# Two sliding-window attention layers and two spatial-shift MLPs on one core: alternating parities over the partitions, one transfer per tile, and most activations turned by a DMA instead of TensorE

## The chip, the cores and the metric

The kernel runs on one core of one Trainium2 chip. The metric is the device time of one execution in microseconds (us); lower is better. Three executions of the kernel before took 1238.16, 1242.08 and 1244.62 us, so its median is 1242.08 us. Everything is read from one profiled execution, whose first instruction starts 1238.3 us before its last one ends.

## The reference, cut to what matters

```python
def A(x):                      # x: [2048, 512]; wqkv [512,1536], wo [512,512]
    q, k, v = split_heads(layernorm(x) @ wqkv)      # 32 heads of 16
    # position s looks at s, s-2, s-4, ..., s-14 (8 of them), masked below 0
    return softmax(q . k[window] / 4) . v[window] @ wo
def B(x):                      # F = 1792
    h = gelu(layernorm(x) @ w1)
    # the four quarters of the features come from positions s-1, s+1, s-2, s+2
    x1 = x + shifted(h) @ w2
    return x1 + gelu(layernorm(x1) @ w3) @ w4
for _ in range(2):
    x = x + A(layernorm(x)) ; x = x + B(layernorm(x))
```

Inputs and outputs are float32. The layer norm stands once in the loop and once more inside A and B; the kernel folds the two into one scale.

## The kernel before, in words

**Work units.** The 2048 positions are cut into 4 blocks of 512 (`NB`), and each block into 4 tiles of 128 positions (`NT`). A unit of the program is a layer and a block, `n` from 0 to 7: 0 to 3 are the blocks of the first pass, 4 to 7 those of the second. A unit goes through five stages:

- `p1_stream(n)` (line 771; the first unit has its own `p1_quarters`, line 727, on plain float32 weights): norm of each tile, the tile turned so that features lie on partitions, then q, k and v by TensorE, evicted to `ev` and written to DRAM (`q_d`, `kv_d`).
- `p2_unit(n, qt)` (line 938): attention for one quarter of the heads: q and k/v are read back from DRAM in a layout in which a partition holds 4 positions of its own and the 7 earlier ones of the window, and VectorE does the products, sums and the softmax. The result `o` is turned into `oT`.
- `p3(n)` (line 1037): `oT` times wo, added to x; norm; the tile turned into `nT`; `nT` times w1, GELU, result `h` with the positions on the free axis, and copies of its edges for the shifts.
- `p4(n)` (line 1153): shifted `h` times w2, added; norm; the tile turned into `x2T` (again a buffer of kind `nT`).
- `p5(n)` (line 1219): 14 chunks of w3, GELU, w4, accumulated in the four `acc` banks of PSUM; the result is added to x and, in the second pass, written out.

**Numbers in two halves.** Except for the first unit, whose weights are used in float32, each float32 operand is held as two float16 numbers, high and low, and every product is three matmuls (`HLS`, line 51: high x high, high x low, low x high). So an activation that has been turned must also be split into a high and a low float16 half.

**Turning a tile.** `turn_pe` (line 644) transposes a 128x512 float32 tile on TensorE, as four 128x128 matmuls with the identity matrix `ident` into one PSUM bank of kind `mm`. `split` (line 667) then has ScalarE copy the bank to float16 (the high half) and VectorE subtract that from the bank (the low half). There are 128 such turns: 4 tiles in each of 8 units at four places, p1, p2 (one for each quarter of the heads), p3 and p4 (7 of them by `turn_f32`, line 656, into plain float32, in the first unit).

**Layout of positions.** In a tile, partitions 0 to 63 hold 64 positions of even parity and 64 to 127 those of odd parity. A transfer between DRAM and such a tile therefore comes as two DMAs of 64 partitions (`dma2`, line 477, `rows`, line 511; the stores of k and v in `p1_stream`, line 798; the output, line 1292). For unit 0, k and v of the first quarter are shifted inside SBUF by small DMAs, and those of the other quarters are copied within SBUF and shifted (lines 952 to 966).

**Order of the work.** Each step is recorded as an operation with its reads, writes and one or more engines that could do it (`op`, line 205). `plan` (line 246) simulates the engines with costs written beside each operation and a list of priorities, `PLACES` (line 57), takes the best operation that is ready, gives buffers from pools (`slots`, line 391), and so fixes the order on every engine; `InOrder` (line 348) keeps the instructions of each engine in that order. All instructions are issued from one helper line, 358, so that the profile tells groups apart by tile names, not by lines. Almost all DMAs are issued by SyncE (SP), in order: a DMA whose buffer is not free yet holds all those behind it.

Of the kernel before, what the change touches and what calls it, by code (L numbers as in the profile page):

```python
# [18 lines left out]
P = 128  # L19
# [11 lines left out]
PAD = W - 1  # L31
NSL = NT + W - 1
# [6 lines left out]

# [4 lines left out]


PLACES = [int(k) for k in """
# [127 lines left out]
""".split()]  # L185


class Buf:

# [11 lines left out]
class Graph:  # L201
# [3 lines left out]
    def __call__(self, key, alts, r=(), w=(), after=(), xfer=0.0):  # L205
# [26 lines left out]
        for p in before:  # L232
            p.succ.append(o)
# [1104 lines left out]
```

## Time and profile before

| what | value |
|---|---|
| times of three executions | 1238.16, 1242.08, 1244.62 us |
| span of the profiled execution | 1238.3 us, 15802 instructions |
| TensorE (PE) busy | 1193.5 us, 5676 matmuls; weight loads 592.2 us beside it |
| VectorE (DVE) busy | 903.5 us |
| ScalarE (ACT) busy | 632.0 us |
| GpSimd (POOL) busy | 372.4 us |
| moved by DMA | 176.71 MB, 143 GB/s over the span |

A group of the profile is read like this: engine, operation, the tile written `<-` the tiles read, shapes, `x`count, then the summed busy time in us and the mean of one in ns, then the idle time of the engine just ahead of them with what ended it. Matmuls overlap in the array, so that their mean duration is longer than the time from one to the next; the price of a matmul in a stream is taken from the starts of neighbours in the timeline. In the chain of waits a piece is a start, a length and what ran or was waited for. The three executions differ by 0.5%.

### The profile page before, as it was taken

The numbers are of one execution on the slowest core, as the hardware profiler recorded it, in microseconds if no ns is written. First come the engines' busy times: TensorE is split into PE (matmuls) and PEld (weight loads), VectorE is DVE, ScalarE is ACT, GpSimd is POOL, SyncE is SP. The second block draws the span as 40 slices with busy tenths as digits, with TensorE's granted clock in tenths as the row PEclk, the third lists the DMA queues.
The fourth block names the chain that finished last, engine by engine and source line by source line (L and its number), as shares of the span: only waits on it lengthen the run. The fifth ranks groups of instructions, "written<-read, shape, count | busy, mean of one in ns | idle before, by whom it ended". The sixth has DMA issues, their size and how long they took to land.

```text
span 1238.3 us, 15802 instructions
## 1 busy us (share of the span) xinstructions
PE 1193.5 (96%) x5676; PEld 592.2 (48%) x5676; DVE 903.5 (73%) x896; ACT 632.0 (51%) x1108; POOL 372.4 (30%) x516
## 2 busy tenths in 40 slices
PE   9977799899999999999999999989999999999998
PEld 7533344455454445444444545444454444444554
DVE  4776998998999989599954998389855888314212
ACT  4645547533774456556543655365543654444431
POOL 6342123402540264147422252051513432121000
PEclk9988899899999999999999999999999999999999
DMA  6565777586666543653348623764157435211322
GB/s 199 160 163 156 220 219 227 161 227 169 195 178 177 132 136 81 151 154 95 109 147 197 162 75 126 202 153 124 60 153 187 124 93 167 68 60 58 88 85 68
DMA packets 129597, 176.71 MB, mean 143 GB/s; under 512 B 11504, under 2 KB 72912, under 8 KB 129520
## 3 DMA queue, kind: packets, MB, share of 16 engines
q1 hardware_dynamic: 127216, 173.78, 50.2%
q10 hardware_dynamic: 2304, 1.95, 0.6%
q8 instruction: 44, 0.72, 0.3%
q14 instruction: 33, 0.27, 0.1%
HBM read 132.64 MB, written 37.87 MB: 138 GB/s over the span
## 4 chain that ended last, share of the span: by engine, by line
PE 76%; DVE 7%; DMA 7%; ACT 3%; POOL 2%; SPq 2%; issue 2%; ACTq 0%; DVEq 0%; POOLq 0%
PE mm L358 54%; PE acc L358 22%; DVE prod L358 3%; SPq L358 2%; DMA kv<-kv_d 2%; DMA kv<-x 1%; DVE L L358 1%; POOL b L358 1%; DMA w<-in_A_x_dram 1%; POOL a L358 1%; DMA h<-in_B_w_dram 1%; ACT junk L358 1%; DMA q<-q_d 1%; ACT ev L358 1%; DMA kv_d<-ev 1%
## 5 line engine op out<-in xcount | busy, mean ns | idle before, releaser
L358 PE MATMUL acc<-w,g 128*128 128x512 f16 (+1 forms) x1260 | 309.0, 394 | 0.0
L358 PE MATMUL mm<-nT,w 128*128 128x512 f16 (+1 forms) x1288 | 305.5, 390 | 1.5 <-ACT nT L358 0.7
L358 PE MATMUL mm<-wq_hl,xt 128*128 128x512 f16 x1008 | 234.8, 389 | 13.3 <-ACT ev L358 11.4
L358 ACT ACTIVATE mm<-mm,s_w 128x512 f32<-128x512 f32 (+1 forms) x144 | 90.6, 629 | 228.8 <-PE mm L358 228.5
L358 PEld LDWEIGHTS <-w 128*128 128x128 f16 x1344 | 124.9, 98 | 137.3 <-issue 1.3
L358 PEld LDWEIGHTS <-g 128*128 128x128 f16 x1176 | 115.1, 98 | 129.9 <-issue 1.1
L358 PEld LDWEIGHTS <-xt 128*128 128x128 f16 x1008 | 100.3, 100 | 133.8 <-issue 23.2
L358 DVE TENSOR_TENSOR prod<-kv,q 128x4096 f32<-128x4096 f32 x29 | 128.6, 4434 | 20.2 <-DMA kv<-kv_d 12.2
L358 DVE TENSOR_TENSOR prod<-kv,L 128x4096 f32<-128x4096 f32 x32 | 141.4, 4418 | 0.6 <-DMA kv<-kv_d 0.3
L358 DVE TENSOR_REDUCE L<-prod 128x256 f32<-128x4096 f32 x32 | 141.2, 4414 | 0.1
L358 DVE TENSOR_TENSOR prod<-prod 128x2048 f32<-128x2048 f32 x64 | 117.5, 1837 | 1.1
L358 POOL TENSOR_TENSOR g<-f,g 128x512 f16<-128x512 f32 x42 | 61.0, 1453 | 189.7 <-ACT g L358 89.4
L358 DVE SCALAR_TENSOR_TENSOR g<-mm,c_g,g 128x512 f16<-128x512 f32 x56 | 41.8, 747 | 75.8 <-ACT g L358 74.1
L358 PE MATMUL mm<-nT,w_hl 128*128 128x512 f16 x384 | 87.8, 379 | 0.0
L358 PE MATMUL mm<-wo_hl,oT 128*128 128x512 f16 x384 | 86.1, 379 | 0.0
L358 PE MATMUL mm<-w_hl,h 128*128 128x512 f16 x384 | 85.0, 379 | 0.0
L358 POOL COPY h<-h 128x126 f16<-128x126 f16 (+3 forms) x56 | 47.4, 869 | 118.1 <-DVE h L358 116.6
L358 PE MATMUL mm<-ident,f 128*128 128x128 f32 x384 | 59.0, 280 | 21.0 <-ACT f L358 16.0
L358 ACT ACTIVATE g<-mm,c_g 128x512 f16<-128x512 f32 x98 | 66.9, 685 | 2.1
L358 PEld LDWEIGHTS mm<-ident,f 128*128 128x128 f32 x384 | 47.2, 143 | 40.2 <-ACT f L358 19.1
L358 ACT ACT_TABLE_LOAD x48 | 61.6, 1283 | 9.0 <-DVE mx L358 5.2
L358 PEld LDWEIGHTS <-oT 128*128 128x128 f16 x426 | 41.7, 98 | 49.4 <-issue 0.6
(159 smaller groups left out, 1365.0 us busy)
## 6 DMA issues: line engine op xcount, KB each, us to landing
w<-w SPq DMA_DIRECT2D x196, 256.0 KB
kv<-kv_d SPq DMA_DIRECT2D x112, 352.0 KB
w<-in_B_w_dram SPq DMA_DIRECT2D x56, 256.0 KB
kv_d<-ev SPq DMA_DIRECT2D x112, 128.0 KB
x<-x SPq DMA_DIRECT2D x32, 256.0 KB
q_d<-ev SPq DMA_DIRECT2D x28, 256.0 KB
w<-g SPq DMA_DIRECT2D x28, 256.0 KB
q<-q_d SPq DMA_DIRECT2D x28, 256.0 KB
```

Of the source, the lines that this page charges most:

```text
L358: i = f(*a, **k).ins
```

## The change

**Parities alternate over partitions.** Partition 2k holds an even and 2k+1 an odd position. A tile of 128 rows is then one access pattern and one DMA, for x, the residual, k and v, and the output:

```diff
-    def rows(ap, b, i, par):
-        r = 512 * b + 2 * i + par
-        v = ap[r:r + 1, 0:D]
-        return bass.AP(tensor=v.tensor, offset=v.offset, ap=[[8 * D, 64], [1, D]])
+    def rows(ap, b, i):
+        v = ap[512 * b + 2 * i:512 * b + 2 * i + 1, 0:D]
+        return at(v, [[8 * D, 64], [D, 2], [1, D]])
```

q, k and v share one DRAM tensor for each pass, `kvq_d`, with 12 planes of 4 + 512 rows of 512 numbers. A k or v tile is read as rows p-4, p-2 and p, so it holds 12 slots of 128 numbers instead of 11, by one DMA instead of two. For unit 0 the quarters 1 to 3 are also written to `kvq_d` and read back; the copies inside SBUF remain for the first quarter alone, three for k and three for v. The edge copies of `h` are strided accordingly.

**Turning by DMA.** A new helper splits first, in SBUF, and turns both halves (128 x 1024 float16, 256 KB) by one transposing DMA from SP's queue:

```diff
+    def turn_dma(key, n, dst, cells, out, rd, scale=None):
+        hl = Buf("g")
...
+        act(key, lambda: A.activation(hv(0), n.t, AF.Copy, scale=sc), rd + k, [(hl, 0), (dst, "new")],
+            also=[(DVE, lambda: V.tensor_scalar(hv(0), n.t, sc, None, ALU.mult), None)])
+        if scale is None:
+            op(key, [(DVE, lambda: V.tensor_sub(hv(1), n.t, hv(0)), None),
+                     (POOL, lambda: G.tensor_sub(hv(1), n.t, hv(0)), None)], [n, (hl, 0)], [(hl, 1)])
+        else:
+            rest(key, lambda: hv(1), lambda: n.t, sc, lambda: hv(0), [n, (hl, 0), scale], [(hl, 1)])
+        op(key, [(SP, lambda: Y.dma_start_transpose(out(), hl.t), None)], [(hl, [0, 1])], hc)
+    MINUS = (1, 2, 3), (0, 1), ()
+    BY_DMA = (4, 5, 6, 7), (2, 3, 4, 5, 6, 7), (1, 2, 3, 4, 5, 6, 7), (2, 3, 4, 5, 6, 7)
```

The four tuples of `BY_DMA` are the units in which p1, p3, p4 and p2 turn by DMA: 16, 24, 29 and 24 turns, 93 of the 128. In `MINUS` stand the units of p1 and p3 (12 and 8 turns) whose turn stays on TensorE with another way to the low half: one more matmul subtracts the high half in the PSUM bank, and ScalarE copies the rest, where VectorE subtracted before:

```diff
+        if minus:
+            act(key, lambda: A.activation(hi(), pv(), AF.Copy), [ps], [hc])
+            pe(key, lambda: T.matmul(pv(), minus_id, hi(), start=False, stop=True, skip_group_check=True), [hc], [ps])
+            act(key, lambda: A.activation(lo(), pv(), AF.Copy), [ps], [lc])
```

**The order.** The simulating `plan`, its costs and `PLACES` go. A list `ORDER` names each operation and the engine that does it, in the order of issue, and `SLOTS` names the buffer of each tile:

```diff
-PLACES = [int(k) for k in """ ...
+ORDER = [int(k) for k in """ ...
+    for k in ORDER:
+        o = ops[k // 4]
+        assert o.before | o.order <= done
+        done.add(o)
+        todo.append(o.alts[k % 4][1])
```

**Smaller edits.** More operations may go to another engine (evictions of q, k and v, squares of the weights, edge copies: also VectorE; norms: also GpSimd or VectorE). The four small GpSimd chains that make the norm's scale in p1 of units 1 to 3 become one. `turnstile` keeps loads of the same line (weights, k and v, q) in order. The pools change: `f32` 6 to 5 buffers, `ev` 3 to 2, `g` 5 to 7. `p3` no longer waits for the last w2 matmul of the unit before; the norm of p4's first tile is ordered after this unit's w1 matmuls, and that of each next tile after the w2 matmuls of the one before.

More of the change, by code (lines that the diff above doesn't have):

```diff
@@ L1 @@
-import heapq
 from contextlib import ExitStack
@@ L30 @@
 W = 8
-PAD = W - 1
-NSL = NT + W - 1
+NSL = NT + W
+BACK = 4
+WARM = 64
 HW = 640
@@ L193, in __init__ @@
         self.kind, self.t, self.cells = kind, t, {}
-        self.users, self.left, self.slot = 0, 0, None
 class Op:
-    __slots__ = ("key", "alts", "succ", "n", "est", "touch", "seq", "fn", "end", "xfer", "eng", "lend")
+    __slots__ = ("alts", "before", "order", "touch", "seq")
 class Graph:
@@ L231, in __call__ @@
         before.discard(o)
-        for p in before:
-            p.succ.append(o)
-        o.n = len(before)
+        o.before, o.order = before, set(after)
         o.touch = [b for b in touch.values() if b.kind is not None]
-        for b in o.touch:
-            b.users += 1
-            b.left += 1
         self.ops.append(o)
         return o
-LAT, LAT_PE, LAT_SP, LAT_DMA, TABLE = 0.12, 0.4, 0.3, 2.3, 1.3
 def plan(ops, slots):
-    free = [0.0] * 5
-    pool = {k: [(0.0, j) for j in range(len(v))] for k, v in slots.items()}
+    bufs, done, todo = {}, set(), []
@@ L340, in plan @@
-    return order
+        for b in o.touch:
+            bufs.setdefault(id(b), b)
+    for b, c in zip(bufs.values(), "".join(SLOTS.split()), strict=True):
+        b.t = slots[b.kind][int(c, 16)]
+    for k in ORDER:
[3 more added lines that the diff above has]
+        todo.append(o.alts[k % 4][1])
+    assert len(done) == len(ops)
+    return todo
 @with_exitstack
@@ L439, in tile_mixer @@
     V.memset(nhalf, -0.5)
-    maskb = const.tile([P, NT, W], F32, name="maskb")
-    G.memset(maskb, 0.0)
-    for base in (0, 64):
-        for i in range(NT):
-            if i < 3:
-                G.memset(maskb[base:base + 2, i, 0:3 - i], -1e9)
-            G.memset(maskb[base:base + 1, i, 0:7 - i], -1e9)
+    junk = const.tile([P, D], BF16, name="junk")
+    zero = slots["prod"][0][:4 * 8, :D]
+    V.memset(zero, 0.0)
     ident = const.tile([P, P], F32, name="ident")
@@ L450, in tile_mixer @@
                     pattern=[[-1, P]], channel_multiplier=1)
-    junk = const.tile([P, D], BF16, name="junk")
-    zero = slots["prod"][0][:16, :PAD * P]
-    V.memset(zero, 0.0)
-    kv_d = [dram.tile([3, 4, 2, PAD + S // 2, P], F32, name=f"kv_d{l}") for l in range(2)]
-    q_d = [dram.tile([4, NB, P, NT, P], F32, name=f"q_d{l}") for l in range(2)]
-    w34_d = [dram.tile([P, 2, 2, 512], F16, name=f"w34_{c}") for c in range(NF)]
-    RS, QS = (PAD + S // 2) * P, 2 * (PAD + S // 2) * P
-    A.dma_start(at(kv_d[1], [[RS, 16], [1, PAD * P]]), zero)
@@ L464, in tile_mixer @@
-    for j in range(len(slots["kv"])):
-        for base in (0, 64):
-            G.memset(slots["kv"][j][base:base + 1, 3 * P:PAD * P], 0.0)
-            G.memset(slots["kv"][j][base:base + 2, :3 * P], 0.0)
+    minus_id = const.tile([P, P], F16, name="minus_id")
+    G.tensor_scalar(minus_id, ident, -1.0, None, ALU.mult)
+    kvq_d = [dram.tile([12, BACK + S // NT, NT * P], F32, name=f"kvq_d{l}") for l in range(2)]
+    w34_d = [dram.tile([P, 2, 2, 512], F16, name=f"w34_{c}") for c in range(NF)]
@@ L468, in tile_mixer @@
+    RS = NT * P
+    QS = (BACK + S // NT) * RS
     kvb = [Buf() for _ in range(2)]
-    qb = [Buf() for _ in range(2)]
     w34 = Buf()
-    def dma(key, out, in_, r, w, xfer, after=(), by_act=False):
-        e, q, d = (ACT, A, 0.6) if by_act else (SP, Y, 0.45)
-        return op(key, [(e, d, lambda: q.dma_start(out(), in_()), None)], r, w, after, xfer)
-    def dma2(key, out, in_, r, w, xfer, after=()):
-        def fn():
-            for par in range(2):
-                Y.dma_start(out(par), in_(par))
-        return op(key, [(SP, 1.15, fn, None)], r, w, after, xfer)
@@ L485, in par_of @@
-    def par_of(t, par):
-        return t[64 * par:64 * par + 64]
-    def act(key, d, fn, r, w, cls=None, after=()):
-        return op(key, [(ACT, d, fn, cls)], r, w, after)
-    def dve(key, d, fn, r, w, lock=False, after=()):
-        return op(key, [(DVE, d, fn, "lock" if lock else None)], r, w, after)
-    def gp(key, d, fn, r, w, after=()):
-        return op(key, [(POOL, d, fn, None)], r, w, after)
-    def pe(key, d, fn, r, w, after=()):
-        return op(key, [(PE, d, fn, None)], r, w, after)
@@ L500, in tile_mixer, with act, dve, gp @@
-    GELU, EXP = "gelu", "exp"
-    xd1 = [dram.tile([P, NT, D], F32, name=f"x1_{b}") for b in range(NB)]
+    def act(key, fn, r, w, cls=None, after=(), also=()):
+        return op(key, [(ACT, fn, cls), *also], r, w, after)
+    def dve(key, fn, r, w, after=(), also=()):
+        return op(key, [(DVE, fn, None), *also], r, w, after)
+    def gp(key, fn, r, w, after=(), also=()):
+        return op(key, [(POOL, fn, None), *also], r, w, after)
+    def pe(key, fn, r, w, after=()):
+        return op(key, [(PE, fn, None)], r, w, after)
@@ new lines, in dma, with turnstile @@
+    def dma(key, out, in_, r, w, after=(), by_act=False):
+        e, q = (ACT, A) if by_act else (SP, Y)
+        return op(key, [(e, lambda: q.dma_start(out(), in_()), None)], r, w, after)
+    before = {}
+    def turnstile(line, *a):
+        before[line] = [dma(*a, after=before.get(line, ()))]
+    GELU, EXP = "gelu", "exp"
+    tiles = list(range(NT))
+    for l in range(2):
+        dma(-8.6, lambda l=l: at(kvq_d[l][0, 0], [[QS, 8], [RS, BACK], [1, RS]]), lambda: zero,
+            [], [(kvb[l], "pad")], by_act=True)
@@ L504, in tile_mixer, with masks @@
+    maskb = keep("maskb", [P, NT, W])
+    def masks():
+        G.memset(maskb.t, 0.0)
+        for i in range(NT):
+            if i < 3:
+                G.memset(maskb.t[0:4, i, 0:3 - i], -1e9)
+            G.memset(maskb.t[0:2, i, 0:7 - i], -1e9)
+    gp(-8.0, masks, [], [maskb])
+    xd1 = [dram.tile([P, NT, D], F32, name=f"res{b}") for b in range(NB)]
     xb = Buf()
@@ L534, in power_of @@
         ps, f2 = Buf("mm"), Buf("mx")
-        pe(key, 0.4, lambda: T.matmul(ps.t[:, :n], ones, ssv, start=True, stop=True), [ss], [ps])
+        pe(key, lambda: T.matmul(ps.t[:, :n], ones, ssv, start=True, stop=True), [ss], [ps])
         def bound():
@@ L542, in bound @@
             V.tensor_scalar(f2.t[:, :m], v, 1e-30, 1e30, ALU.max, ALU.min)
-        dve(key, 0.35, bound, [ps], [f2])
-        p = inv.t[:, :m] if inv.kind is None and not isinstance(inv.t, tuple) else inv.t
-        gp(key, 0.6, lambda: G.tensor_tensor(p, f2.t[:, :m], nhalf[:, :m], ALU.pow), [f2], [inv])
+        dve(key, bound, [ps], [f2])
+        p = inv.t[:, :m]
+        gp(key, lambda: G.tensor_tensor(p, f2.t[:, :m], nhalf[:, :m], ALU.pow), [f2], [inv])
         def cut():
@@ L629, in fn, with powers, normed, turn @@
             G.tensor_scalar(nb.t[:, s], tot.t[:, k:k + 1], r.t[:, s], c, ALU.mult, ALU.mult)
-        gp(key, 1.0, fn, [(ss, j), (tot, k)], [(ve, i), (r, i), (nb, i)])
+        gp(key, fn, [(ss, j), (tot, k)], [(ve, i), (r, i), (nb, i)])
+    def powers(key, ss, ve, r, c1, c2, tot, nb):
+        def fn():
+            G.tensor_scalar(ve.t, ss.t, c1, c2, ALU.mult, ALU.add)
+            G.tensor_tensor(r.t, ve.t, nhalf, ALU.pow)
+            G.tensor_tensor(nb.t, tot.t, r.t, ALU.mult)
+            G.tensor_scalar(nb.t, nb.t, C0, None, ALU.mult)
+        gp(key, fn, [(ss, tiles), (tot, tiles)], [ve, (r, tiles), (nb, tiles)])
     C0 = -1.0 / D
     C1 = 1.0 / D ** 3
-    def normed(key, n, src, r, nb, i, rd, new=(), also=()):
+    def normed(key, n, src, r, nb, i, rd, new=(), after=()):
         s = slice(i, i + 1)
         f = lambda e: (lambda: e.tensor_scalar(n.t, src(), r.t[:, s], nb.t[:, s], ALU.mult, ALU.add))
-        op(key, [(ACT, 0.82, lambda: A.activation(n.t, src(), AF.Identity, bias=nb.t[:, s],
-                                                  scale=r.t[:, s]), None),
-                 *[(e, d, f(q), c) for e, d, q, c in also]],
-           rd + [(r, i), (nb, i)], [n, *new])
-    def turn_pe(key, n, dst, cells, hi, lo, rd, new=(), scale=None):
+        op(key, [(ACT, lambda: A.activation(n.t, src(), AF.Identity, bias=nb.t[:, s],
+                                            scale=r.t[:, s]), None),
+                 (POOL, f(G), None), (DVE, f(V), None)], rd + [(r, i), (nb, i)], [n, *new], after)
+    def turn(key, n, dst, rd):
         ps = Buf("mm")
@@ L651, in fn @@
                 f = slice(P * c, P * (c + 1))
-                T.transpose(ps.t[:, f], n.t[:, f], ident)
-        pe(key, 0.44, fn, rd, [ps, (dst, "new"), *new])
-        split(key, ps, dst, cells, hi, lo, scale)
-    def turn_f32(key, n, dst, cell, out):
-        ps = Buf("mm")
-        def fn():
-            for c in range(NC):
-                f = slice(P * c, P * (c + 1))
-                T.transpose(ps.t[:, f], n.t[:, f], ident)
-        pe(key, 0.44, fn, [n], [ps, (dst, "new")])
-        act(key, 0.6, lambda: A.activation(out(), ps.t.rearrange("p (c t) -> p c t", c=NC), AF.Copy), [ps], cell)
@@ L667, in split @@
-    def split(key, ps, dst, cells, hi, lo, scale=None):
-        hc, lc = [(dst, [(c, a) for c in cells]) for a in range(2)]
-        pv = lambda: ps.t.rearrange("p (c t) -> p c t", c=NC)
-        if scale is None:
-            act(key, 0.6, lambda: A.activation(hi(), pv(), AF.Copy), [ps], [hc])
-            dve(key, 0.69, lambda: V.tensor_sub(lo(), pv(), hi()), [ps, hc], [lc])
-        else:
-            act(key, 0.72, lambda: A.activation(hi(), pv(), AF.Copy, scale=scale.t), [ps, scale], [hc])
-            dve(key, 0.75, lambda: V.scalar_tensor_tensor(
-                lo(), pv(), scale.t, hi(), ALU.mult, ALU.subtract), [ps, hc, scale], [lc])
+                T.matmul(ps.t[:, f], n.t[:, f], ident, is_transpose=True, start=(c == 0), stop=(c == NC - 1))
@@ L679, in tile_mixer, with xt_view @@
+    def turn_f32(key, n, dst, cell, out):
+        ps, pv = turn(key, n, dst, [n])
+        act(key, lambda: A.activation(out(), pv(), AF.Copy), [ps], cell,
+            also=[(DVE, lambda: V.tensor_copy(out(), pv()), None)])
     both = [(0, 0), (0, 1)]
+    PLAIN = 1
+    MINUS = (1, 2, 3), (0, 1), ()
+    BY_DMA = (4, 5, 6, 7), (2, 3, 4, 5, 6, 7), (1, 2, 3, 4, 5, 6, 7), (2, 3, 4, 5, 6, 7)
     lb = [(l, b) for l in range(2) for b in range(NB)]
     N = len(lb)
-    STATS = 1
+    def xt_view(xt):
+        return xt.t.rearrange("p (a c t) -> p a c t", a=2, c=NC)
@@ new lines, in p1_stats @@
+    def p1_stats(n, key):
+        l, b = lb[n]
+        tot, ss, ve, r, nb = [s[n % SC] for s in stat["a"]]
+        k = SN ** -2
+        for i in range(NT):
+            x = xs[0, b, i] if l else xin[0, b, i]
+            src = lambda x=x: x.t if l else f32v(x.t, D)
+            if l == 0:
+                act(key, lambda src=src, i=i: A.activation(
+                    junk, src(), AF.Identity, accum_out=tot.t[:, i:i + 1]), [x], [(tot, i)])
+            t = x_sum[b] if l else tot
+            sq_dev(key, src, t, ss, i, [x])
+            if l:
+                power(key, ss, ve, r, i, C1 * k, EPS * k, t, C0, nb)
+        if l == 0:
+            powers(key, ss, ve, r, C1 * k, EPS * k, tot, nb)
@@ L768, in p1_quarters @@
+            for j in range(2):
+                r0 = P - BACK if qt == 0 else 0
+                dma(-4.4 + 0.1 * qt, lambda j=j, qt=qt, r0=r0: at(
+                    plane(0, j, qt, BACK + r0), [[RS, P - r0], [1, RS]]),
+                    lambda kv=kv, j=j, r0=r0, first=first: kv[j].t[r0:P, first:first + RS],
+                    [(kv[j], tiles)], [(kvb[0], [(0, i, qt, j) for i in range(NT)])])
         first_q["done"] = done
@@ L1058, in fn @@
                         m += 1
[L1059 to L1060 removed]
+            pe(key + 0.01 * i, fn, [*[(t, both) for t in oTs[n]], x, (wo, whole)], [ps])
             src = lambda x=x: x.t
[L1062 removed]
+            dve(key, lambda ps=ps, src=src, s=s: V.scalar_tensor_tensor(
                 src(), ps.t, s_wo.t, src(), ALU.mult, ALU.add, accum_out=sums.t[:, s]),
@@ L1282, in down @@
                                      start=(c == 0 and j == 0), stop=(c == NF - 1 and j == 2))
-                pe(key, 0.65 * (k1 - k0), down, [w4, (g, [0, 1])], acc[k0:k1])
-        for k, (m, i) in enumerate(tiles):
+                pe(key, down, [w4, (g, [0, 1])], acc[k0:k1])
+        for k, (m, i) in enumerate(grp):
             l, b = lb[m]
@@ L1291, in p5 @@
             if l:
-                for p in range(2):
-                    dma(base, lambda b=b, i=i, p=p: rows(out_d, b, i, p),
-                        lambda x=x, p=p: par_of(x.t, p), [x], [], 0.4, by_act=n == N - 1 and p == 1)
+                dma(base, lambda b=b, i=i: rows(out_d, b, i), lambda x=x: x.t, [x], [], by_act=n == N - 1 and k % 2)
     p2(0)
```

624 lines of the change are left out of this document (264 added, 360 removed), and 266 rows, old and new, of tables (ORDER, PLACES).

## The prediction

> **What bounds the kernel now.** I read the page first: busy times, the slices, the chain that ended last.
>
> ```profile
> PE 1193.5 (96%) x5676; PEld 592.2 (48%) x5676; DVE 903.5 (73%) x896; ACT 632.0 (51%) x1108; POOL 372.4 (30%) x516
> ...
> PE   9977799899999999999999999989999999999998
> DVE  4776998998999989599954998389855888314212
> PEclk9988899899999999999999999999999999999999
> PE 76%; DVE 7%; DMA 7%; ACT 3%; POOL 2%; SPq 2%; issue 2%; ACTq 0%; DVEq 0%; POOLq 0%
> ```
>
> TensorE is the bound: 96% busy, 76% of the chain. The holes are in the first fifth, where the slices of PE show 7 and the granted clock 8. Busy times of four stretches size them (PE busy is the second number, the granted clock stands ahead of the DMA share):
>
> ```profile
> 0.00:240.00 240.00, 208.60 (x938) 112.04 (x939) 188.83 (x208) 138.02 (x295) 84.96 (x142) 0.94 0.66 186
> 240.00:480.00 240.00, 237.17 (x1021) 117.12 (x1020) 220.43 (x211) 126.42 (x213) 73.34 (x104) 1.00 0.61 169
> 480.00:1120.00 640.00, 633.98 (x3060) 305.17 (x3058) 462.65 (x423) 329.24 (x527) 208.56 (x255) 0.99 0.47 129
> 1120.00:1238.30 118.30, 113.78 (x662) 57.83 (x660) 31.64 (x57) 38.30 (x76) 5.57 (x15) 0.99 0.24 74
> ```
>
> PE idles 31.4 us of the first 240, 2.8 of the next 240, 6.0 of the 640 after that and 4.5 at the end. From 240 us on the kernel ends earlier almost only by less PE work. VectorE is at 92% from 240 to 480 us and at 72% from there to 1120.
>
> **The turns that leave TensorE.** The groups of the transposes, and a stretch of PE's timeline:
>
> ```profile
> L358 PE MATMUL mm<-ident,f 128*128 128x128 f32 x384 | 59.0, 280 | 21.0 <-ACT f L358 16.0 <-ACT ev L358 4.4 <-POOL f L358 0.7
> L358 PE MATMUL mm<-ident,o 128*128 128x128 f32 x128 | 19.3, 273 | 0.0
> ```
>
> ```profile
> 785.77 0.60 PE L358 MATMUL mm<-ident,f 128*128 128x128 f32 x4
> 786.21 2.75 PE L358 MATMUL acc<-w,g 128*128 128x512 f16 x12
> 788.80 0.60 PE L358 MATMUL mm<-ident,f 128*128 128x128 f32 x4
> 789.23 7.93 PE L358 MATMUL mm<-wq_hl,xt 128*128 128x512 f16 x36
> 797.00 5.34 PE L358 MATMUL mm<-wo_hl,oT 128*128 128x512 f16 x24
> ```
>
> 512 transposes are 128 turns of four. The price is not the mean of 280 ns, which overlaps the neighbours, but start to start: 785.77 to 786.21 and 788.80 to 789.23, 0.435 us for a turn. A 512-column matmul costs (797.00 - 789.23) / 36 = 0.216 us. The tuples of the diff send 16 + 24 + 29 + 24 = 93 turns to the DMA: 93 x 0.435 = 40.5 us leave PE. The 20 turns with the subtracting matmul add 20 x 0.216 = 4.3 us. All the other matmuls stay. So PE's queue gets 36.2 us shorter, and as PE runs without holes where nearly all these turns stand, the end moves by that unless new holes come.
>
> [...]
>
> **What the turned tiles cost instead.** The splits change engine input, not their number:
>
> ```profile
> L358 ACT ACTIVATE nT<-mm 128x512 f16<-128x512 f32 (+1 forms) x63 | 36.9, 590 | 25.2 <-PE mm L358 25.1
> L358 DVE TENSOR_TENSOR nT<-mm,nT 128x512 f16<-128x512 f32 x60 | 40.3, 685 | 34.1 <-ACT nT L358 34.1
> L358 ACT ACTIVATE g<-w,inv_p 128x512 f16<-128x512 f32 x18 | 12.4, 715 | 2.1 <-DVE oT L358 0.8 <-DMA w<-g 0.7 <-DVE inv_p L358 0.6
> L358 DVE SCALAR_TENSOR_TENSOR g<-w,inv_p,g 128x512 f16<-128x512 f32 x28 | 20.7, 780 | 0.0
> L358 POOL TENSOR_TENSOR g<-f,g 128x512 f16<-128x512 f32 x42 | 61.0, 1453 | 189.7 <-ACT g L358 89.4
> ```
>
> The weights' split is the nearest row for a split within SBUF: 0.715 us on ScalarE against 0.590, and 0.780 on VectorE against 0.685. 93 x 0.22 = 20 us over two engines with 600 and 330 us to spare; hidden beside PE, so nothing. The subtracting matmul takes 20 x 0.685 = 14 us off VectorE and gives 12 us to ScalarE, which is free as well. Where GpSimd takes a low half it is 1.45 us, on an engine that is 30% busy.
>
> No transposing DMA runs in the kernel before, so its cost has to be bounded. Its rate first, and what issuing costs SP:
>
> ```profile
> q1 hardware_dynamic: 127216, 173.78, 50.2%
> L358 SPq DMA_DIRECT2D w<-w x196: 319/320/1534, 314.9 to 1210.5; - x196
> L358 SPq DMA_DIRECT2D kv<-x x30: 517/682/1572, 41.5 to 110.8; - x30
> kv<-kv_d SPq DMA_DIRECT2D x112, 352.0 KB
> kv_d<-ev SPq DMA_DIRECT2D x112, 128.0 KB
> ```
>
> The queue moves 173.78 MB in 50.2% of 1238.3 us = 622 us, 0.28 MB per us. 93 x 262,144 bytes = 24.4 MB are 87 us at that rate, 7% more load on engines about half free; four times slower would be 28%, still room on average after 480 us, where the share is 0.47. Below nothing it can't be, as the bytes are new. SP issues 93 more DMAs of 0.32 to 0.68 us (30 to 63 us), but fewer of the others: the 112 and 112 quoted become 62 and 56, 96 loads of x and the residual and stores of the output become 48, and some 40 of unit 0's small copies go: about 194 less. So SP has no more to do than before, if a transposing DMA is issued like these.
>
> Its latency, from the chain of waits (the DMA pieces of three stretches):
>
> ```profile
> 45.81 10.81 DMA kv<-x
> ...
> 58.25 6.87 DMA kv<-x
> ```
>
> ```profile
> 456.38 4.69 DMA x<-x
> ```
>
> ```profile
> 931.37 2.53 DMA kv_d<-ev
> ...
> 937.91 8.71 DMA kv<-kv_d
> ```
>
> From issue to landing that is 2.5 us (128 KB) up to 10.8 (256 KB behind others). I take 4.7, the row of the same size on a queue after the start. A hand-off before is 0.435 + 0.590 + 0.685 = 1.7 us; after it is 0.715 + 0.780 + 4.7 = 6.2, so 4.5 us later, with ends of 2.3 and 10.6. [...]
>
> Who waits: PE, in a fixed order, and behind its waiting matmul all other PE work. The cover is the matmuls of other stages put between (w3/w4 chunks of the unit before, q/k/v of a later one), and it is thick: PE idles 6.0 us in the 640. It is out at the places where PE runs dry today:
>
> ```profile
> 461.26 0.66 PE L358 MATMUL mm<-ident,f 128*128 128x128 f32 x4 [1.80 <-ACT f L358]
> ```
>
> ```profile
> 829.33 0.89 PE L358 MATMUL mm<-ident,f 128*128 128x128 f32 x4 [2.79 <-ACT ev L358]
> ```
>
> ```profile
> 959.77 1.12 PE L358 MATMUL mm<-ident,f 128*128 128x128 f32 x4 [2.60 <-ACT f L358]
> ```
>
> Each time the wait ends with a norm in front of a turn. There I count the full 4.5 us: 3 x 4.5 = 13.5 us back, with ends of 0 and 3 x 10.6 = 32.
>
> **The start.** The chain from 0 to 240 us, by line:
>
> ```profile
> by line: PE mm L358 24.2%; SPq L358 8.7%; DVE prod L358 8.7%; DMA kv<-x 7.4%; issue 6.9%; DMA w<-in_A_x_dram 5.7%; POOL a L358 3.6%; DMA h<-in_B_w_dram 3.5%; ACT junk L358 3.1%; DVE g L358 2.1%; DMA kv<-kv_d 2.1%; DMA w<-in_B_w_dram 2.0%; A
> ```
>
> SP's issuing is 8.7% of 240 = 20.9 us of it. One DMA for a tile instead of two, and no shifted copies for three quarters of unit 0, halve that: 10.4 us off. Against it, unit 0's k and v now go to DRAM and back; write and read by the rows 2.5 and 8.7 are 11.2 us in place of one copy of 6.9 or 10.8, about even, so nothing. One GpSimd chain for four and more choice of engines could recover more; the end is half the stretch's loss, (31.4 idle + 240 x 0.06 clock) / 2 = 23 us. The other end is 10 us lost to the DRAM trips.
>
> **Sum.** 1238.3 - 40.5 + 4.3 + 13.5 - 10.4 = 1205.2 us of span. The median of the executions is 3.8 us above the profiled span (1242.08), so 1209 us. With the ends of latency and start (13.5 less to 18.5 more, 12.6 less to 20 more), taking one end at a time, this case alone reaches from 1195 to 1229.
>
> **Rivals.**
>
> Everything is hidden. If the order fills the three dry places and the start gives back 23 us: 1242.1 - 36.2 - 23 = 1183 us. For it: DMA engines and three other engines have room. Against: VectorE at 92% from 240 to 480, which sets when attention is ready, and so how early PE's cover comes.
>
> Thin cover. Units 2 to 7 each have three turns in series (oT, nT, x2T), 18 hand-offs, and the kernel as a whole has 36.2 us less PE work for cover. If each shows 1.2 us of its 4.5 that gives 1242.1 - 36.2 + 18 x 1.2 = 1227 us. For it: only the order of the list protects PE, and nothing in the trace says how that list weighs a DMA's landing.
>
> Slower: transposing DMAs land late. A 256 KB DMA among others took 10.8 us; a turned one, written in much smaller pieces, could take that or more every time, or hold SP while it is issued, with the loads of weights and k/v behind it. If half of the 18 hand-offs show 10.6 us: 1242.1 - 36.2 + 95 = 1301. It decides from 36.2 / 18 = 2.0 us shown per hand-off. For it: the queue is in order, and k and v loads of 768 KB stand in it. Against: with a DMA share of 0.47 and VectorE at 72% from 480 us on, queue and cover have room there. [...]
>
> That the change does not do what it says is not likely here: the diff names the turns that leave PE.
>
> **Chances.** Forecast 0.50, everything hidden 0.17, thin cover 0.16, late transposes 0.17. About 0.5% (6 us) is what a measurement of this kernel can tell from no change. Faster by more than that, below 1236: all of the first two and 0.12 of the third, 0.79. Within: 0.04 of thin cover and 0.02 of the last, 0.06. Slower: 0.15. For 8 in 10 I leave out most of the last rival and the lower half of the second's spread: 1180 to 1246 us.
>
> **What would show it right or wrong.** PE's transposes fall from 512 to 35 x 4 = 140, with 20 matmuls on `minus_id`; PE busy falls by about 36 us plus what holes it loses. If the forecast holds, PE stays at 95% or more and the DMA of `nT`, `xt` and `oT` ends few of PE's waits, 15 us or less in sum. If DMA pieces of these tiles show in the chain with over 36 us, the slower rival is right. If PE's idle time in the first 240 us stays at 31, the 10 us of the start were wrong; if SP's time for one transposing DMA is far above 0.7 us, the cost of issuing was.

## The result, and the profile after

The change made the kernel slower, by half a per cent: 1247.37 us (median of 10 executions, 1242.97 to 1251.77) against 1241.67 for the kernel before (10 executions beside it), a ratio of 1.0054 with an interval of 1.0035 to 1.0073. The forecast was 1209. The profiled execution of the kernel after spans 1245.8 us. Its busy times:

```profile
PE 1166.2 (94%) x5324; PEld 551.6 (44%) x5324; DVE 955.5 (77%) x990; ACT 586.0 (47%) x984; POOL 441.7 (35%) x502
...
PE   9769999899698999999999998999899999889997
...
PEclk9979999899999999999999998999999999999999
```

The matmuls that were to go did go: 5324 in place of 5676, and PE is busy 27.3 us less. But from the eleventh slice on six slices of PE show 6 or 8 where before they showed 9, and the mean granted clock is 0.977 (0.985 before). The four stretches (PE busy is the second number) give the sizes:

```profile
0.00:240.00 240.00, 209.90 (x961) 114.13 (x962) 207.84 (x227) 119.36 (x240) 72.64 (x97) 0.95 0.61 189
240.00:480.00 240.00, 218.69 (x875) 101.84 (x875) 216.67 (x223) 126.41 (x213) 106.74 (x110) 0.98 0.64 188
480.00:1120.00 640.00, 618.19 (x2815) 276.71 (x2814) 500.98 (x487) 304.21 (x461) 249.16 (x275) 0.98 0.60 164
1120.00:1245.80 125.80, 119.43 (x678) 58.91 (x675) 30.03 (x54) 36.01 (x72) 13.21 (x21) 0.99 0.30 91
```

PE idles 30.1, 21.3, 21.8 and 6.4 us, 79.6 in all, where it idled 31.4, 2.8, 6.0 and 4.5. So 34.8 us of new idle time stand against 27.3 us of work saved: 7.5 us more span. What PE waits for (us in total, times, longest):

```profile
PE mm L281 <- DVE h L281: 20.3, 9, 4.1
PE mm L281 <- ACT w_hl L281: 13.1, 2, 11.5
...
PE mm L281 <- DMA xt<-g: 3.8, 1, 3.8
...
PE mm L281 <- DMA nT<-g: 1.3, 1, 1.3
```

The turned tiles `xt` and `nT` hold PE up for 5.1 us, all 93 together. The largest wait is one that the kernel before did not have: VectorE's writing of `h`, the hidden values of the shifting MLP between w1 and w2. The two groups that store `h` show why:

```profile
L281 ACT ACTIVATE h<-mm,c_h 128x512 f16<-128x512 f32 x32 | 51.7, 1614 | 14.1 <-POOL h L281 12.6 <-DVE h L281 0.7
L281 DVE SCALAR_TENSOR_TENSOR h<-mm,c_h,h 128x512 f16<-128x512 f32 x32 | 51.0, 1625 | 36.8 <-ACT h L281 36.5 <-POOL h L281 0.2
```

In the kernel before, the same 32 stores took 686 ns each on ScalarE and 745 on VectorE:

```profile
L358 DVE SCALAR_TENSOR_TENSOR h<-mm,c_h,h 128x512 f16<-128x512 f32 x32 | 23.5, 745 | 20.5 <-ACT h L358 20.5
L358 ACT ACTIVATE h<-mm,c_h 128x512 f16<-128x512 f32 x32 | 21.8, 686 | 0.7
```

Shapes and counts are the same; a mean hides that half of the stores are as before and half take about 2.55 us on ScalarE and 2.5 on VectorE. One place in PE's timeline, and VectorE's in the same stretch (start, us, what, and in brackets the idle time ahead with what ended it):

```profile
749.78 2.75 PE L281 MATMUL mm<-nT,w_hl 128*128 128x512 f16 x12
753.64 5.34 PE L281 MATMUL mm<-nT,w_hl 128*128 128x512 f16 x24 [1.11 <-DVE h L281]
763.11 2.29 PE L281 MATMUL mm<-w_hl,h 128*128 128x512 f16 x5 [4.13 <-DVE h L281]
```

```profile
751.11 2.48 DVE L281 SCALAR_TENSOR_TENSOR h<-mm,c_h,h 128x512 f16<-128x512 f32 x1
...
754.76 4.42 DVE L281 TENSOR_TENSOR prod<-kv,L 128x4096 f32<-128x4096 f32 x1
759.40 3.66 DVE L281 SCALAR_TENSOR_TENSOR h<-mm,c_h,h 128x512 f16<-128x512 f32 x3 [0.22 <-POOL h L281]
```

A store of 2.48 us holds the PSUM bank that the next w1 matmuls need (PE starts 0.05 us after it ends), and the last stores, behind a 4.4 us attention product, come late for w2.

The lines of the change that do this are in `p3`. They write two of the four groups of channels so that later a contiguous read of 128 columns gives the rows shifted by one:

```diff
-            hi, lo = [lambda a=a, g=g: hb()[:, a, g, OWN[g]:OWN[g] + D] for a in range(2)]
...
+            def to(a, g=g):
+                v = blocks(h.t, HW)[:, a, g]
+                if g < 2:
+                    return at(v[:, 1:], [list(v.ap[0]), [P, NT], [2, 64], [P - 1, 2]])
+                return v[:, P:] if g == 2 else v[:, :D]
```

With even and odd positions side by side, each value goes 254 bytes on from the one before, or 250 back, in turn (the innermost step is 127 float16).

### The profile page after: what moved, and what is told of

The parts are those of the page before. It is cut to its first block, busy times and chain, and to the rows that moved or that the text cites. A ratio compares the mean times of both kernels' runs of the same rounds, so it can differ in the third digit from the quotient of the medians.

```text
span 1245.8 us, 15079 instructions
## 1 busy us (share of the span) xinstructions
PE 1166.2 (94%) x5324; PEld 551.6 (44%) x5324; DVE 955.5 (77%) x990; ACT 586.0 (47%) x984; POOL 441.7 (35%) x502
## 5 line engine op out<-in xcount | busy, mean ns | idle before, releaser
L281 PE MATMUL mm<-wq_hl,xt 128*128 128x512 f16 x1008 | 229.4, 384 | 8.5 <-DMA xt<-g 3.8
L281 POOL TENSOR_TENSOR g<-f,g 128x512 f16<-128x512 f32 x80 | 126.7, 1589 | 197.4 <-ACT g L281 98.1
L281 PE MATMUL mm<-nT,w_hl 128*128 128x512 f16 x384 | 93.5, 397 | 18.5 <-DVE h L281 10.8
L281 PE MATMUL mm<-w_hl,h 128*128 128x512 f16 x384 | 90.9, 393 | 9.1 <-DVE h L281 8.2
L281 POOL TENSOR_SCALAR b<-b 128x1 f32<-128x1 f32 (+1 forms) x48 | 28.4, 591 | 155.4 <-ACT junk L281 153.4
L281 POOL COPY h<-h 128x126 f16<-128x126 f16 (+3 forms) x40 | 37.2, 949 | 128.0 <-DVE h L281 102.2
L281 DVE SCALAR_TENSOR_TENSOR h<-mm,c_h,h 128x512 f16<-128x512 f32 x32 | 51.0, 1625 | 36.8 <-ACT h L281 36.5
L281 PEld LDWEIGHTS <-w_hl 128*128 128x128 f16 x384 | 38.7, 101 | 70.5 <-issue 29.1
L281 PEld LDWEIGHTS <-h 128*128 128x128 f16 x384 | 38.5, 101 | 58.4 <-issue 16.9
```

What stands on the lines that cost most here:

```text
L281: i = f(*a, **k).ins
```

## The experiments

Three theories. T1: the interleaved stores of `h` cost the gain. T2: the DMA turns cost it, by landing, issue or load. T3: the new order of the work is thinner, that is, it leaves PE less other work to cover a wait, whatever the stores do. All ratios below are to the kernel before.

**The stores in plain order.** The kernel after, with these lines changed (and the edge copies for two rows in every group):

```diff
-                if g < 2:
-                    return at(v[:, 1:], [list(v.ap[0]), [P, NT], [2, 64], [P - 1, 2]])
-                return v[:, P:] if g == 2 else v[:, :D]
+                return v[:, P:] if g % 2 == 0 else v[:, :D]
...
-                return ps.t.rearrange("p (i k r) -> p i k r", i=NT, r=2) if g < 2 else ps.t
+                return ps.t
```

> The kernel after, with h of the MLP stored in the order in which the matmuls give it (512 adjacent float16) for all four groups of channels, not only for the two that shift by two. The groups that should shift by one row then shift by two, so half of the channels of h are read one row off. Nothing else is changed: same order, same DMA turns. Theory T1 (the interleaved stores of h cost the gain: 16 of 32 stores on ScalarE and on VectorE take 2.55 us in place of 0.69 and 0.74, and PE waits 20.3 us for VectorE's h): all 64 stores are back at 0.69 and 0.75 us, PE's wait on VectorE for h falls from 20.3 us to under 4, the clock returns to 0.985, and the time is 1215 to 1228 us. Theory T2 (the DMA turns cost it, by their landing, SyncE's issue time or the DMA load): 1240 to 1248 us. Theory T3 (the order of the work is thinner at the start and elsewhere, whatever the stores do): 1232 to 1242 us, since the 30 us without PE in the first 240 us stay.

Measured: 1211.86 us, ratio 0.9737 (0.9699 to 0.9774). The stores are back at 686 and 746 ns, the clock at 0.985. T1 holds, 3 us below its own range; T2 and T3 had put it at 1232 or more. All 93 turns by DMA are still in this kernel, so their landing, their issue and their bytes are not what the 36 us went for.

**The same stores, another walk.** Only the order of the loops differs:

```diff
-                    return at(v[:, 1:], [list(v.ap[0]), [P, NT], [2, 64], [P - 1, 2]])
+                    return at(v[:, 1:], [list(v.ap[0]), [P - 1, 2], [2, 64 * NT]])
...
-                return ps.t.rearrange("p (i k r) -> p i k r", i=NT, r=2) if g < 2 else ps.t
+                return ps.t.rearrange("p (m r) -> p r m", r=2) if g < 2 else ps.t
```

> The kernel after with nothing of the computation changed: the same interleaved stores of h, walked in another order. After walks row by row, so that each write lies 254 bytes from the one before; here all even rows go first and then all odd rows, so that each write lies 4 bytes from the one before, and PSUM is read at every second float32. If the distance between writes in SBUF sets the price, the strided stores fall from 2.55 us to 0.7 to 0.9 us, and by T1 the time is 1215 to 1230 us. If any 2-byte write that isn't adjacent to the last costs this, or if PSUM's stride costs as much as SBUF's, they stay at 1.6 us or more and the time at 1238 to 1250. By T2 the time stays at 1240 to 1248 whatever the stores do.

Measured: 1211.64 us, ratio 0.9755 (0.9724 to 0.9786), again 3 us below the range. This computes all that the kernel after computes, with the same instructions in the same order, and is 35.7 us faster than it and 30 us faster than the kernel before: the best version here. Its groups, and PE's largest waits:

```profile
L281 DVE SCALAR_TENSOR_TENSOR h<-mm,c_h,h 128x512 f16<-128x512 f32 x32 | 24.4, 767 | 22.3 <-ACT h L281 22.0 <-POOL h L281 0.2
L281 ACT ACTIVATE h<-mm,c_h 128x512 f16<-128x512 f32 x32 | 24.3, 761 | 4.6 <-POOL h L281 3.5
```

```profile
PE mm L281 <- ACT w_hl L281: 12.8, 2, 11.6
PE mm L281 <- DMA w<-w: 4.7, 2, 3.8
...
PE mm L281 <- DVE h L281: 3.1, 2, 2.9
PE mm L281 <- DMA xt<-g: 3.0, 1, 3.0
...
PE mm L281 <- DMA nT<-g: 1.6, 1, 1.6
```

The wait for VectorE's `h` fell from 20.3 to 3.1 us. The span is 1210.2 us and PE is busy 1156.7 of it. So of the 35.6 us between the two spans 26.1 are idle time of PE (79.6 against 53.5), and 9.5 are longer busy time for the same 5324 matmuls, at a granted clock of 0.977 against 0.984.

**The turns without turning.** One line of the kernel after:

```diff
-        op(key, [(SP, lambda: Y.dma_start_transpose(out(), hl.t), None)], [(hl, [0, 1])], hc)
+        op(key, [(SP, lambda: Y.dma_start(out(), hl.t.rearrange("p (k t) -> p k t", t=P)), None)], [(hl, [0, 1])], hc)
```

> The kernel after with each of the 93 transposing DMAs replaced by a plain DMA of the same 256 KB, with the same source, target, queue and place in the order; the tiles are then not turned, so that what is computed from them is not the reference's. T1: the transposing of the DMA is no cost, PE's waits for VectorE's h stay at about 20 us, and the time is 1240 to 1250 us. [...]

Measured: 1247.27 us, ratio 1.0046 (1.0028 to 1.0063), the kernel after's time within 0.1 us. So the turning as such costs nothing here; the plain copies land no sooner (3.2 us against 3.3 for `nT`) and move the same bytes, so this run doesn't test landing and load. As the slow stores could have hidden a cost of the turning, the same edit was made to the kernel with the swapped loops:

> The kernel with the swapped loops, with each of the 93 transposing DMAs replaced by a plain DMA of the same 256 KB at the same place; the tiles are not turned, so that what is computed from them is not the reference's. T1: PE waits 4.6 us in all for the turned tiles, and plain DMAs land no sooner (3.2 against 3.3 us), so 1208 to 1214 us. T2 in a weaker form (the transposing costs something that the slow stores hid): 1205 us or less, since SyncE's issue falls from 1.25 to 0.60 us each.

Measured: 1211.72 us, 0.9757 (0.9737 to 0.9778): again no difference, though SyncE's time for issuing a turn is about halved. SyncE's rows (ns least, median and most of one), first of the kernel after, then of the kernel after with plain copies:

```profile
L281 SPq DMA_TRANSPOSE nT<-g x52: 1231/1247/3332, 369.7 to 1136.4; - x52
```

```profile
L281 SPq DMA_DIRECT2D nT<-g x52: 593/604/1221, 370.3 to 1137.8; - x52
```

**The stores alone, in the kernel before.** Turns on PE, its own layout and order; the stores of two groups scattered:

```diff
+                if g < 2:
+                    return at(v[:, OWN[g]:], [list(v.ap[0]), [1, 256], [256, 2]])
...
```

> The kernel before (turns on PE, its own order) with one thing added: the stores of h of the two groups that shift by one row are scattered, even columns into the first 256 places and odd columns into the last 256, so that each 2-byte write lies 512 bytes from the one before; half of the channels of h are thus read at wrong rows. T1: 16 of 32 stores on each of ScalarE and VectorE take about 2.5 us in place of 0.69 and 0.74, PE waits on VectorE's h where it did not before, and the time rises from 1242 to between 1257 and 1275 us. T2: at most 4 us above the kernel before, since PE has work beside these stores.

Measured: 1261.04 us, ratio 1.0152 (1.0122 to 1.0181), 19.4 us above the kernel before. The stores take 1612 and 1625 ns on average, as in the kernel after. So the price does not need the change's order; the kernel after shows more of it (35.7 us). It is not all seen as a wait for `h`: PE's wait for VectorE's `h` is 3.9 us here, while its wait for the norm's tiles from ScalarE (`f`) rises from 16.0 to 22.6 us. Longer stores also delay other work on their engines.

**One engine at a time.** From the kernel with the swapped loops, first ScalarE's stores back to the far walk (`far=True`), then VectorE's:

```diff
+                if g < 2 and far:
+                    return at(v[:, 1:], [list(v.ap[0]), [2, 64 * NT], [P - 1, 2]])
```

> The kernel with the swapped loops, but with ScalarE's stores of the upper halves of h (16 of 32) walked as in the kernel after, each write 254 bytes from the one before; VectorE's stores keep the swapped loops, and nothing of the computation changes. T1 with a chain (GELU, then ScalarE's store, then VectorE's, then PE, one after the other): about half of the 36 us between 1211.6 and 1247.4 comes back, 1222 to 1236 us. If only VectorE's stores matter (PE is seen to wait for VectorE): at most 1216 us. If only ScalarE's queue matters, behind which the GELUs wait: over 1240 us.

> The kernel with the swapped loops, but with VectorE's stores of the lower halves of h (16 of 32) walked as in the kernel after, each write 254 bytes from the one before; ScalarE's keep the swapped loops, and nothing of the computation changes. Both engines' far stores together cost 35.8 us (1247.4 against 1211.6), ScalarE's alone 10.8. If the two prices add, 1234 to 1240 us. If each alone finds some cover that the two together don't, 1218 to 1228 us. If VectorE is the one that PE waits for whatever ScalarE does, over 1240.

Measured: 1222.45 us (0.9846, 0.9831 to 0.9861) for ScalarE, 1231.73 us (0.9925, 0.9893 to 0.9956) for VectorE: 10.8 and 20.1 us above the kernel with the swapped loops, 30.9 in sum, against 35.7 for both. The prices nearly add, as in a chain: ScalarE's was within its range, at the low end, and VectorE's is 2 us below the range for adding and 4 above the one for cover. The far walk gives each engine 27 us more work (51.7 - 24.3 and 51.0 - 24.4), so some 40% of ScalarE's shows and three quarters of VectorE's, which is the busier one and the last in the chain. Both together cost 5 us more than the sum; the executions of one of these kernels alone spread over 11 us (1225.54 to 1236.44), so that this is not shown to be more than noise.

**A price list.** In units 0 to 3 writes in SBUF 4, 8, 16 and 32 bytes apart, in units 4 to 7 reads of PSUM 8 to 64 bytes apart:

```diff
+                v = v[:, P:] if g % 2 == 0 else v[:, :D]
+                return v.rearrange("p (k r) -> p r k", r=2 << g) if n < 4 else v.rearrange("p (r k) -> p r k", r=2 << g)
...
```

> A price list, from one profile: the kernel with h stored in the order of the matmuls (all shifts by two, so half of the channels of h are read one row off), in which moreover the 512 values of each row of h are permuted on their way from PSUM to SBUF, so that the sums that use h are not the reference's. In units 0 to 3 PSUM is read in order and consecutive writes in SBUF lie 4, 8, 16 and 32 bytes apart (groups g = 0, 1, 2, 3); in units 4 to 7 SBUF is written in order and consecutive reads of PSUM lie 8, 16, 32 and 64 bytes apart. [...] T1b (the price grows with the distance): four steps, each dearer. T1c (only PSUM in order is cheap): the second half of the list is dear, the first cheap; the loops swapped, which read PSUM 8 bytes apart at 0.76 us, speak against it.

One execution, 1222.28 us; it was run for its durations. ScalarE's timeline in unit 0, then in unit 4:

```profile
184.93 0.83 ACT L281 ACTIVATE h<-mm,c_h 128x512 f16<-128x512 f32 x1
...
188.77 1.41 ACT L281 ACTIVATE h<-mm,c_h 128x512 f16<-128x512 f32 x1
...
194.55 2.54 ACT L281 ACTIVATE h<-mm,c_h 128x512 f16<-128x512 f32 x1
...
198.09 2.47 ACT L281 ACTIVATE h<-mm,c_h 128x512 f16<-128x512 f32 x1
```

```profile
745.79 0.69 ACT L281 ACTIVATE h<-mm,c_h 128x512 f16<-128x512 f32 x1
...
750.97 0.69 ACT L281 ACTIVATE h<-mm,c_h 128x512 f16<-128x512 f32 x1
...
754.16 0.69 ACT L281 ACTIVATE h<-mm,c_h 128x512 f16<-128x512 f32 x1
...
756.15 0.69 ACT L281 ACTIVATE h<-mm,c_h 128x512 f16<-128x512 f32 x1
```

4, 8, 16 and 32 bytes cost 0.83, 1.41, 2.54 and 2.47 us (VectorE: 0.79, 1.36, 2.49, 2.40), where adjacent values cost 0.69 and 0.75; PSUM's walks cost nothing (0.69 us on ScalarE, 0.73 to 0.75 on VectorE). From 16 bytes on the price is flat up to the 254 and 512 bytes of the kernels above (2.53 to 2.56 us on ScalarE at 254; at 512 the mean of 1612 ns, with half of the stores at 686, makes 2.54). So T1b, the price that grows with the distance, holds up to 16 bytes and not beyond, and T1c is wrong: part of the first half of the list is dear and nothing of the second. Up to 16 bytes each byte of distance costs ScalarE (1.41 - 0.83) / 4 = 0.145 us and then (2.54 - 1.41) / 8 = 0.141 us; why the price stops growing there is not shown. VectorE also reads the high half of `h` from SBUF in the same walk, which is not separated from its write.

**The other half of the change, transfers of whole tiles.** The kernel with the swapped loops, its transfers of x, the output, q/k/v and the windows in two again, partitions 0 to 63 and 64 to 127, as in the kernel before:

```diff
+        def fn():
+            for k in range(2):
+                q.dma_start(out(k), in_(k))
...
+    hf = lambda t, k: t[64 * k:64 * k + 64]
```

> The kernel with the swapped loops, with the transfers of the change undone in number: each load of x, each store of the output, each store of q, k and v and each load of a k or v window goes in two DMAs of 64 partitions in place of one of 128; nothing of the computation changes. If one transfer per tile is worth something on the path (the prediction took 10.4 us for the start), the time rises from 1211.6 to between 1217 and 1225 us, and PE's idle time in the first 240 us from 27.5 to over 31. If SyncE's issues lie beside other work, the time stays within 1208 to 1215 us.

Measured: 1276.84 us, 1.0273 (1.0249 to 1.0297): 65 us lost, far beyond what either side expected. Three parts of it:

> The kernel with the swapped loops, with only the loads of x and the stores of the output in two DMAs of 64 partitions each (the kernel with all transfers in two took 1276.8 us against 1211.6). Nothing of the computation changes. It adds 46 issues of SyncE of 0.59 us, 27 us in all, most of them in the first 130 us. If the loads of x are what the start waits for (the prediction's 10.4 us), 1218 to 1228 us with PE's idle time in the first 240 us at 33 or more; if they lie beside other work, 1209 to 1215.

> The kernel with the swapped loops, with each store of q, k and v and each load of a k or v window in two DMAs that each keep all 128 partitions and the same runs of bytes; loads of x are whole. Nothing of the computation changes. The number of DMAs is as in the kernel with all transfers in two, but a DMA of 128 partitions takes SyncE 0.37 us and one of 64 took 0.60. Theory S (SyncE's issue time sets the price, 65 us for 157 us more of it): 55 us more of it, so 1225 to 1240 us. Theory D (64 partitions hold up the DMA engines: their share rose from 58.8 to 65.8 per cent): 1210 to 1218 us. Theory N (the number of DMAs, whatever they cost SyncE): 1245 us or more.

> The kernel with all transfers in two DMAs of 64 partitions, with the 93 transposing DMAs replaced by plain ones of the same 256 KB; the tiles are not turned, so that what is computed from them is not the reference's. SyncE's issue time falls by 63 us (from 493 to about 430) while the number of DMAs stays. Theory S: 1245 to 1260 us. Theory D: 1265 to 1277 us, since the halves stay. Without the splits the same replacement was worth nothing (1211.7 against 1211.6).

Measured: 1226.99 us (0.9881, 0.9853 to 0.9909) with x and the output alone in halves, so 15.4 us, of which 5.9 are idle time of PE in the first 240 us (33.4 against 27.5; only 16 of the 46 added issues lie in the first 130 us, the rest are loads of residuals and stores of the output); 1214.81 (0.9774, 0.9748 to 0.98) with twice as many DMAs of 128 partitions for q/k/v and windows, so 3.2 us, for 81 us more of SyncE's issue; 1271.20 (1.0231, 1.02 to 1.0262) with all halves but plain copies for turns, 5.6 us back for 66 us less issue. The second and third are in the ranges of Theory D. If the parts add, the lower and upper halves of q/k/v and the windows are some 50 of the 65 us; they were not run alone. Last, which 64 partitions:

```diff
-    hf = lambda t, k: t[64 * k:64 * k + 64]
+    hf = lambda t, k: t[k::2]
```

> The kernel with the swapped loops, with the same transfers in two as in the kernel that took 1276.8 us (loads of x, stores of the output, of q, k and v, loads of the windows), but one DMA takes the 64 even partitions and the other the 64 odd ones, in place of the lower and the upper 64. Nothing of the computation changes. [...] Theory D2 (a DMA of 64 partitions is dear for SyncE or the queues, whichever partitions they are): 0.6 us of issue each, and 1260 to 1280 us.

Measured: 1235.72 us (0.9963, 0.9942 to 0.9985), 41 us better than the lower and upper halves and 24 worse than whole tiles: well below the range of Theory D2, so that it does matter which partitions they are. The queue's share of the 16 DMA engines in the kernel with the swapped loops, with lower and upper halves, and with even and odd ones:

```profile
q1 hardware_dynamic: 238088, 204.04, 58.8%
```

```profile
q1 hardware_dynamic: 241160, 204.05, 65.8%
...
kv<-kvq_d SPq DMA_DIRECT2D x124, 384.0 KB, 5.6
```

```profile
q1 hardware_dynamic: 241160, 204.05, 58.6%
...
kv<-kvq_d SPq DMA_DIRECT2D x124, 384.0 KB, 4.9
```

Of spans of 1210.2, 1276.0 and 1237.2 us that is 712, 840 and 725 us of packet time for the same bytes, 16 engines at a time, and 48, 56 and 48 ns for a packet on average. Lower and upper halves cost the DMA engines 18% more, even and odd ones 2%; why is not shown. What the remaining 24 us are stays open. SyncE issues 153 us more there, but 81 us more cost only 3.2 us above. Nor is it the 64 partitions alone that make an issue long. SyncE's rows, first two of the kernel with the swapped loops, then one of that with lower and upper halves:

```profile
L281 SPq DMA_DIRECT2D kvq_d<-ev x84: 359/370/1650, 80.0 to 907.5; - x84
L281 SPq DMA_DIRECT2D x<-in_A_x_dram x16: 534/557/1134, 120.7 to 521.3; - x16
```

```profile
L281 SPq DMA_DIRECT2D kvq_d<-ev x168: 574/608/2075, 86.6 to 967.0; - x168
```

A store of q, k or v takes SyncE 0.37 us whole and 0.61 in a half of 64 partitions, but a whole load of x over 128 partitions takes 0.56 as well; its DRAM side is walked as 64 pairs of rows. All of this is in an order fixed for whole tiles; what halves cost in an order planned for them is open.

## Why the prediction was wrong, step by step

**The step that failed** is "as PE runs without holes where nearly all these turns stand, the end moves by that unless new holes come", with the paragraph that begins "The splits change engine input, not their number" as the only price of work on ScalarE and VectorE. The new address pattern of `h` was in the diff and has no term in the sum: it was put at nothing without a reason. It kept number, shape and bytes of 32 stores on each engine and made 16 of them longer, by 1.86 us on ScalarE and 1.76 on VectorE; the runs put it at 35.7 us (1247.4 against 1211.6), which is nearly all of the 38 us between forecast and result. None of the rivals has it: the slower one was a late DMA. The same paragraph takes work on these engines as hidden because they have 600 and 330 us to spare; 27 us more on one of them cost 10.8 and 20.1 us, since PE waits for these stores, or for what stands behind them. A reader of the diff could have asked of each changed store how far apart its writes lie.

**The turns, 40.5 - 4.3 = 36.2 us off PE:** right. With the holes of `h` gone PE is busy 1156.7 us, 36.8 less than before.

**The landing, 4.7 us and 13.5 us exposed:** too dear. The DMA view of the kernel after (median us to landing):

```profile
nT<-g SPq DMA_TRANSPOSE x52, 3.3
```

For `oT` and `xt` it is 3.5; 5.1 us in all show, within the limit of 15 that the prediction set. That, and the 1211.64 us of a kernel with all its turns by DMA, refute the slower rival, late transposes; the plain copies land as late and could not.

**SyncE, 0.32 to 0.68 us a turn:** too cheap, 1.25. Summing count times median over SyncE's rows gives 357 us before and 336 after: the 93 turns add 116 us, whole-tile transfers take off more. So SP has indeed no more to do than before, though not for the reason that was given with it, a transposing DMA issued like the others.

**The start, 10.4 us off:** not seen. Idle time in the first 240 us went from 31.4 to 30.1 us, and to 27.5 with the swapped loops, 3.9 at most. There PE now stands 11.6 us behind one small matmul of w1's scale, whose square on ScalarE waits for w1's load and for x's sums; that is read from the timeline, not tested. Loads of x do matter in this order (15.4 us when they and the output go in halves), but that price is not what the change gained over the kernel before.

**The sum.** 1205.2 us of span stands against 1210.2 with the swapped loops: there PE does 36.8 us less and idles 8.7 us more than before (53.5 against 44.8), in place of the forecast's 3.1 (13.5 - 10.4). Between 240 and 480 us it idles 12.9 us in place of 2.8: 3.8 for a weight load, 3.0 for a turned `xt`, 3.0 for ScalarE's halves of `nT`. So the 1209 was about right for a kernel that differs from the change by the order of two loops, but in part by luck: the landing was priced some 9 us too dear and the start at least 6 too generous, and these cancel.

## What to carry to other kernels

Price each changed access pattern, not only added and removed instructions: ask how far apart in SBUF the writes of a store lie, as 512 adjacent float16 cost 0.69 us here and the same values 16 bytes or more apart 2.5. If a layout needs interleaving, let the innermost loop run over the nearest addresses in SBUF, and take the stride on the PSUM side, where it cost nothing here (0.69 us at 8 to 64 bytes). Spare time on an engine hid only a part of added work here (27 us more cost 10.8 us on ScalarE and 20.1 on VectorE): look at what PE waits for. A layout that gives a DMA all 128 partitions was worth more here than the DMAs it saves (65 us lost with all transfers in lower and upper halves, 3.2 with those of q/k/v and windows in as many DMAs of 128 partitions), and a large saving on the bound engine is only seen once the holes that came with it are named.

## What the runs showed of the hardware that was not expected

- A store of 512 2-byte values takes ScalarE 0.69 us and VectorE 0.75 where they are adjacent in SBUF, 0.8 at 4 bytes apart, 1.4 at 8 and 2.4 to 2.65 from 16 to 254 bytes; on ScalarE that is 0.14 to 0.145 us for each byte of distance between 4 and 16. Reads of PSUM 8 to 64 bytes apart cost nothing (0.69 and 0.73 to 0.75 us).
- Issuing a transposing DMA of 256 KB holds SyncE 1.25 us, a plain one with the same target 0.60 (`nT`) or 0.50 (`oT`, `xt`); both land in 3.1 to 3.5 us.
- With q/k/v, windows, x and output in DMAs of the lower and the upper 64 partitions, the DMA engines spend 18% more time on the same bytes of the queue (840 us against 712); with even and odd partitions 2% (725). A DMA of 64 partitions of q, k or v holds SyncE 0.61 us and a whole one 0.37, but a whole load of x 0.56.
